# A fused attention and token-mixing kernel: one scaling product split, mix and projection steps of batch 0 and 2 reordered, a relu moved to GpSimd, three transposes in another tiling

## The chip, the cores and the metric

One core of one Trainium2 chip. The core has TensorE (PE, with its weight loads as PEld), VectorE (DVE), ScalarE (ACT), GpSimd (POOL) and SyncE (SP, which here issues every DMA). The metric is the device time of one execution in microseconds; a kernel's time is the median of its runs.

## The reference

Inputs are q, k and v of shape (8 batches, 8 heads, 576 positions, 64), and three weights. Everything is float32 outside the kernel. Per batch and head, a linear attention with a cosine weighting:

```python
def phi(x, c, s):                 # c, s = cos and sin of pi/2 * position / 576
    r = np.maximum(x, 0.0)
    return np.concatenate([r * c, r * s], axis=-1)
kv = np.einsum('bhsf,bhsd->bhfd', phi(k), v)
z = np.sum(phi(k), axis=2)
num = np.einsum('bhsf,bhfd->bhsd', phi(q), kv)
den = np.einsum('bhsf,bhf->bhs', phi(q), z)[..., None] + 1e-06
x = num / den                     # then (8, 576, 512): the heads side by side
```

and on x, per batch, a mixing of the positions and a projection:

```python
wq = x @ w_q;  wk = x @ w_k       # 512 -> 64
W_tok = scale * np.einsum('bsd,btd->bst', wq, wk)
mixed = np.einsum('bst,btd->bsd', W_tok, x)
out = np.maximum(mixed, 0.0) @ w_out
```

## The kernel before

The program is a list of steps in one string, `ORDER` (lines 26 to 67), which is read from left to right (lines 555 to 568). A word is a step's kind, a number, and up to three marks: `a` or `b` for one half of the data, `:n` for the first of the PSUM banks that it writes (for the steps of TensorE; OE's `:n` is an output buffer), `@A`, `@V` or `@G` for the engine (ScalarE, VectorE, GpSimd). So `KV6:2` is KV of group 6 into banks 2 and 3. Each engine executes its own steps in the order of the string; the steps of different engines are tied by semaphores where they share data, a buffer or a bank. Nothing is planned at run time.

The attention runs over 16 groups H, each with two pairs of heads (half a batch). For group H:

- LK, LQ, LV load k, q and v (line 145) into one of five raw buffers each, in halves of 288 KB.
- RK and RQ are the relus with a cast to bf16 (lines 203 and 205), CV casts v (209, 211).
- VS multiplies v by the cosine and sine table on VectorE (line 234; the tables and v both lie in SBUF). VG does the same on GpSimd straight from the raw data (248). Both write `v2`.
- KV contracts relu(k) with that product on TensorE (275 for the groups in `KV_WIDE`, 285 for the others), KE brings it to SBUF.
- QT transposes relu(q) on TensorE. For the groups in `QT_WIDE` (line 107) it is nine transposes of 128x128 (295), for the others 18 of 64 rows (301), with another layout in PSUM. QM multiplies the result by the q table on VectorE, as two products for a wide group (316) and as one for the others (320).
- N (two per group, 2H and 2H+1) multiplies by KV's result (340; some add the epsilon with two small matmuls, 348). EP, RC or RJ make the reciprocal of the denominator (357, 359, 378, 381), and X multiplies (393) and writes x.
- XT or XR transposes x on TensorE: XT with ten transposes of 128x128 (406), XR with 20 of 64 rows (419). XE brings the result to SBUF (213 on VectorE, 209 on ScalarE).

Per batch b, WK and WQ project (439, 452), KW and QW bring the results to SBUF, KX contracts x with wk (466), XK, XA and XB put it into place, and four mix products MX 4b to 4b+3 (489) follow, each with its evacuation and relu ME (500, 502). WO multiplies by w_out (509), OE brings the block of 128 rows to SBUF, ST stores it. KX of batch 2 uses the same buffers as that of batch 0, so the four MX of batch 0 come before XK2.

PSUM has eight banks. Most steps take a pair of them (`:0`, `:2`, `:4`, `:6`), WK, WQ, KX and WO a single one. A step of TensorE waits until the last step that used its banks has been read, so a bank number in `ORDER` is a dependency. Around the change, before it:

- MX6 4, XT4 0, MX7 2, QT6 6, N15 4, MX3 2, N14 0, WK2 6, WQ2 7, KV6 2, KX2 7, N13 2, N12 0, XR7 4, WO8 6 is TensorE's order with its banks. KV7, ahead of MX6, has banks 2 and 3, N8's, which X8 reads.
- VectorE: VS7, EP8, EP9, RJ4, X8, X9, QM7 (two), XE4, QM6 (two), VS6a, RC14, RC15, X14, X15, CW5, EP13, XK2.
- ScalarE: CV7a, KE4, RQ7a, ME5, ME4, RQ6a, XE5, KE7, ME6, ME7, RK6a, EP15, RK6b, ME3, KW2, QW2, KE6.
- GpSimd: CV7b, RQ7b, RK7, XB1, RQ6b, VG6b, CV6a, CV8a, CW4, CV8b, RQ8a, RK8a, RQ9a, RQ9b, RK9a, RK9b, VG11a. RK8b is on ScalarE.
- Near 56 us: KV8 into bank 0, KV9 into 6, MX9 into 4, MX11 into 0, N16 into 2, WQ3 into 6.

Of the kernel before, what the change touches and what calls it, by code (L numbers as in the profile page):

```python
# [27 lines left out]
LQ2a LK2a LW0 LV2a LQ2b LK2b TB TI TK TZ TQ RQ1a@G TW TV CV1@A VS1b RQ1b@A VS1a T2 QT1:0 RK1a@A  # L28
RK1b@V RQ0@V KV1:2 QM1 QT0:4 KE1@A CV0@G LV5b LV5a RK0@A LK5b LK5a LQ5a LQ5b LQ4b LQ4a N2:2 VS0 N3:0
VG3 QM0 KV0:6 KE0@A RC3 EP2@A X3 RQ3@A N0:6 N1:4 RC2 EP0@V EP1@V X2 RK3@A QT3:0 RC0 XT1:2 X0 XE1@A  # L30
RC1 X1 VG2b KV3:6 QM3 XR0:4 KE3@A CW1@A N6:0 XE0@V EP6@A N7:6 CW0@G EP7@A WK0:4 VG2a RQ2@A WQ0:5
KW0@V RC6 KX0:4 X6 RK2@A LK7a LV4a LV4b LK4a LK4b LV7a LV7b LQ7b LQ7a LQ6a LK7b LV6b LQ6b LW2 LK6b
LK6a LV6a LV8a LW3 LW4 LW5 LQ8b QT2:2 RC7 X7 CV5@A KV2:0 XK0@V QM2 XB0@G QW0@A XT3:6 KE2@A RK5@A
VS5a N5:0 WU5:2 N4:2 VS5b XE3@A RQ5@G EP5@V KV5:4 RC5 RC4 X5 XA0@A X4 QT5:6 KE5@A RQ4@G LQ9b LV8b
LQ8a MX0:0 QM5 XR2:2 ME0@A QT4:4 XE2@A N10:0 QM4 MX1:6 CV4@G LV9b LK8a LQ9a LV9a EP10@A ME1@A WK1:2
WQ1:3 RC10 KW1@A VS4 RK4@A LK9a LK8b LK9b KX1:2 MX2:6 N11:4 XK1@V QW1@A ME2@A EP11@V KV4:2 XA1@A
RC11 X10 CV7a@A CV7b@G X11 MX5:6 MX4:0 KE4@A RQ7b@G RQ7a@A VS7 N8:2 N9:4 ME5@A ME4@A QT7:6 RK7@G
EP8@V EP9@V RJ4 RQ6a@A XT5:0 X8 XB1@G XE5@A X9 KV7:2 RQ6b@G QM7 VG6b MX6:4 KE7@A XT4:0 ME6@A MX7:2
XE4@V QT6:6 ME7@A N15:4 QM6 RK6a@A MX3:2 N14:0 CV6a@G LV11a EP15@A RK6b@A WK2:6 ME3@A VS6a WQ2:7
KW2@A RC14 KV6:2 RC15 QW2@A X14 CV8a@G KX2:7 KE6@A CW4@G X15 CW2@A N13:2 CW3@A CW5@V N12:0 EP13@V  # L40
XR7:4 XK2@V WO8:6 RC13 XA2@A X13 EP12@A CV8b@G XE7@A WO2:7 RC12 VS8 WO7:2 CV9b@A RQ8a@G LQ13a LQ11b
LQ10a LK11b LK11a LQ11a LV11b X12 OE8:0@A MX8:4 WO6:3 RQ8b@A RK8a@G ME8@V OE7:1@A XR6:0 RQ9a@G WO1:6
CV9a@A XE6@V RQ9b@G OE2:2@A QT8:4 VS9 OE6:3@A RK8b@A QT9:0 RK9a@G OE1:4@A WK3:3 QM9 WO4:2 RK9b@G
KW3@A OE4:5@A ST4 LV12a LK10a LQ10b LV10a LV10b LQ12a KV8:0 QM8 XB2@A KV9:6 KE8@A MX9:4 KE9@A MX11:0
VG11a N16:2 ME9@A ME11@V WQ3:6 RC16 KX3:7 X16 QW3@A MX10:0 XK3@A N17:4 ME10@A N19:2 RK11@V N18:6
EP19@A WO11:0 EP17@V RQ11@A RC17 EP18@V X17 WO5:1 VG11b OE11:6@V ST11 LK12a LK10b LQ13b LV12b LK12b
LQ12b QT11:4 OE5:5@A RC19 RC18 X18 WO9:0 X19 WO10:1 OE9:7@A RQ10@G KV11:2 XA3@A QM11 XR8:6 KE11@A
XR9:4 VG10a LV15a LV13a LQ14b LV14b LQ14a LV13b XE8@A QT10:2 XE9@V WO0:5 QM10 OE10:8@A MX13:0
OE0:6@A MX12:6 N22:2 WO12:4 RQ13a@G ME12@V EP22@A XB3@A ME13@A RC22 VG10b WK4:5 X22 MX14:0 KW4@A
N23:6 ME14@V MX15:2 EP23@A KX4:5 RK10@A WQ4:0 XK4@V RQ13b@G RC23 WO3:1 ME15@A X23 XA4@G XB4@A QW4@A  # L50
RQ12b@G KV10:2 OE3:9@V RQ12a@A QT13:6 OE12:10@A ST12 LK13b LK13a LV14a VG12 MX18:0 WO14:5 QM13
KE10@A ME18@A XR11:2 OE14:11@A MX16:0 N21:6 XE11@V ME16@A N20:4 EP21@A EP20@V RK12@A QT12:0 RJ10 X21
WO16:2 RQ14b@A X20 WO13:3 QM12 VG13 XR10:4 OE13:10@A ST13 LK15b LK14b LK14a LV15b ST2 KV12:6 MX19:0
ME19@A WO17:3 OE16:12@A KE12@V XE10@V MX17:0 OE17:13@A N25:6 ME17@V N24:4 RQ14a@A WK5:3 EP25@V
# [16 lines left out]
def kernel(  # L71
# [32 lines left out]
    NUM_JOINT = ()  # L104
    WARM_COLS = 384
    VG_SPLIT = ()
    QT_WIDE = (0, 1, 2, 3, 4, 5, 6, 7, 8, 9, 10, 11, 14)
    KV_WIDE = (2, 4, 5, 7)

    pool = ctx.enter_context(tc.tile_pool(name="sb", bufs=1))  # L110
# [87 lines left out]
    A, V, G = nc.scalar, nc.vector, nc.gpsimd  # L198
# [59 lines left out]
    def qt_wide(i):  # L258
        return pair(i).rearrange("p t e -> p (t e)").bitcast(BF16)[:, 0:C * P].rearrange(
            "p (c n) -> p c n", c=C)  # L260
# [29 lines left out]
    def QT(H, ps, eng):  # L290
        place["QT", H] = ps
        if H in QT_WIDE:
            qt_v = qt_wide(ps)
# [18 lines left out]
    def QM(H, ps, eng):  # L312
        if H in QT_WIDE:
            q_t = qt_wide(place["QT", H]).rearrange("p c (r d) -> p r c d", r=2)
            for r in range(2):
                V.tensor_mul(  # L316
                    qm_b[H % NQM][:, :, r, 0:C, :],
                    q_t[:, r].unsqueeze(1).to_broadcast([P, 2, C, H2]), qtab)
            return
        V.tensor_mul(  # L320
            qm_b[H % NQM][:, :, :, 0:C, :].rearrange("p s r c d -> p s r (c d)"),
            qt_view(place["QT", H]).unsqueeze(1).to_broadcast([P, 2, 2, S]),
            qtab.rearrange("p s c d -> p s (c d)").unsqueeze(2).to_broadcast([P, 2, 2, S]))
# [275 lines left out]
```

## Time and profile before

| | |
|---|---|
| median of 3 runs | 119.17 us (118.6 to 119.84) |
| the profiled execution | 118.42 us |
| its span | 116.6 us |
| granted TensorE clock | 1.0 |
| DMA, share of 16 engines | 92.4% for the one queue of loads and stores |

The profile shows one execution. Times are in us from the start of the span. A row of a timeline has the start, the duration, the engine, the source line, the operation, output and inputs by name, shapes and the number of instructions merged, and in brackets the idle time of the engine ahead of it with the step that ended last before it began. The chain of waits follows back from the last instruction what released each step; its rows have start, duration, engine, name and line. Line numbers are those of the kernel below. The engines overlap the start of a step with the end of the one before by up to 0.1 us, so durations in a row add up to a little more than the time they take together.

### The profile page before, as it was taken

Reading aid. Unit: us, or ns where it says so; the run is one execution under the profiler, and the core shown is the slowest. Engines: PE = TensorE matmul, PEld = TensorE weight load, DVE = VectorE, ACT = ScalarE, POOL = GpSimd, SP = SyncE. Lnnn points to the kernel's source line nnn. Section 1 sums busy time; section 2 is a strip of 40 time slices with the busy share of each in tenths; the row PEclk is TensorE's granted clock in tenths of the full one; section 3 lists DMA queues with packets and bytes.
Section 4 is the critical chain, followed back from the end, with each engine's and each line's share of the span. In section 5 each row is a group of like instructions: output and inputs, shape, how many; then the busy total and the mean of one; then the engine's idle time right before and its main releaser. Section 6 shows DMA issues by size and latency. Waiting matters only on the chain.

```text
span 116.6 us, 4971 instructions
## 1 busy us (share of the span) xinstructions
PE 94.7 (81%) x2104; PEld 65.1 (56%) x2118; DVE 90.5 (78%) x162; ACT 83.1 (71%) x147; POOL 64.8 (56%) x65
## 2 busy tenths in 40 slices
PE   0005967779796797999999899999999999999970
PEld 0004856657576776647775656656775576463420
DVE  2008999799798999889799887898997996795620
ACT  4547558499899987898884878986888774546340
POOL 7600399861634796477298498899659901002000
PEclk9999999999999999999999999999999999999999
DMA  3999999999999999999979999987898467999874
GB/s 90 349 386 399 401 372 346 388 389 396 386 392 384 387 387 387 391 390 384 383 251 302 351 397 371 358 266 258 270 340 293 169 236 271 403 367 400 337 306 173
DMA packets 20662, 39.38 MB, mean 338 GB/s; under 512 B 3232, under 2 KB 3232, under 8 KB 20640
## 3 DMA queue, kind: packets, MB, share of 16 engines
q1 hardware_dynamic: 20640, 39.07, 92.4%
q8 instruction: 16, 0.26, 0.9%
q14 instruction: 6, 0.05, 0.1%
HBM read 29.62 MB, written 9.44 MB: 335 GB/s over the span
## 4 chain that ended last, share of the span: by engine, by line
PE 48%; DMA 26%; DVE 14%; SPq 4%; issue 3%; ACT 1%; DVEq 0%; ACTq 0%
PE ps L509 24%; DMA qraw<-in_q_dram 16%; DMA vraw<-in_v_dram 5%; DMA kraw<-in_k_dram 5%; PE ps L340 5%; DVE qm L316 5%; SPq L145 4%; PE ps L285 3%; PE ps L489 3%; PE ps L419 3%; PE ps L439 3%; DVE xT L213 3%; PE ps L466 3%; PE ps L452 2%; DVE x L393 2%
## 5 line engine op out<-in xcount | busy, mean ns | idle before, releaser
L248 POOL TENSOR_TENSOR v<-vraw,vtab 128x1152 bf16<-128x1152 f32 (+1 forms) x12 | 35.5, 2969 | 6.5 <-DVE qm L316 2.2
L509 PE MATMUL ps<-wow,mix 128*128 128x512 bf16 x130 | 33.3, 380 | 1.2 <-issue 0.3
L393 DVE TENSOR_TENSOR x<-ps,rec 128x640 bf16<-128x640 f32 x32 | 25.4, 818 | 0.7
L209 ACT COPY o<-ps 128x512 f32<-128x512 f32 x25 | 14.5, 592 | 9.2 <-PE ps L509 8.1
L509 PEld LDWEIGHTS <-mix 128*128 128x128 bf16 x144 | 12.5, 98 | 14.4 <-issue 1.7
L295 PE MATMUL ps<-ident,rq 128*128 128x128 bf16 x117 | 9.5, 233 | 12.0 <-ACT rq L203 11.0
L316 DVE TENSOR_TENSOR qm<-ps,qtab 128x1152 bf16<-128x1152 bf16 x26 | 18.3, 749 | 0.8 <-PE ps L295 0.7
L234 DVE TENSOR_TENSOR v<-vb,vtab 128x2304 bf16<-128x2304 bf16 (+1 forms) x11 | 11.8, 1084 | 7.7 <-ACT vb L209 7.3
L500 ACT ACTIVATE mix<-ps 128x576 bf16<-128x576 f32 x23 | 14.5, 651 | 3.5 <-PE ps L489 2.5
L340 PE MATMUL ps<-kvs,qm 64*128 64x65 bf16 x640 | 14.0, 193 | 2.1 <-ACT kvs L209 1.3
L295 PEld LDWEIGHTS <-rq 128*128 128x128 bf16 x117 | 7.6, 104 | 13.6 <-issue 10.5
L340 PEld LDWEIGHTS <-qm 64*128 64x128 bf16 x640 | 12.6, 96 | 4.2 <-issue 2.3
L203 ACT ACTIVATE rk<-kraw 128x1152 bf16<-128x1152 f32 (+1 forms) x14 | 14.0, 996 | 0.7 <-DMA kraw<-in_k_dram 0.7
L205 POOL TENSOR_SCALAR rq<-qraw 128x576 bf16<-128x576 f32 (+1 forms) x13 | 10.1, 776 | 4.4 <-DMA qraw<-in_q_dram 3.5
L211 POOL TENSOR_SCALAR vb<-vraw 128x576 bf16<-128x576 f32 (+1 forms) x7 | 5.7, 810 | 11.9 <-DMA vraw<-in_v_dram 8.8
L211 POOL TENSOR_SCALAR kx<-kx 64x256 bf16<-64x256 bf16 x9 | 4.1, 457 | 12.6 <-ACT kx L209 11.0
L502 DVE TENSOR_SCALAR mix<-ps 128x576 bf16<-128x576 f32 x9 | 6.8, 757 | 4.0 <-PE ps L489 3.8
L285 PE MATMUL ps<-v,rk 64*64 64x130 bf16 x432 | 9.1, 231 | 0.8 <-POOL v L248 0.7
L209 ACT CAST kvs<-ps 128x260 bf16<-128x260 f32 (+1 forms) x15 | 6.5, 436 | 4.6 <-PE ps L285 3.9
L285 PEld LDWEIGHTS <-rk 64*64 64x64 bf16 x432 | 7.5, 114 | 3.9 <-issue 1.2
L203 ACT ACTIVATE rq<-qraw 128x576 bf16<-128x576 f32 (+1 forms) x10 | 8.3, 832 | 1.1 <-DMA qraw<-in_q_dram 1.1
L213 DVE COPY xT<-ps 128x1280 bf16<-128x1280 bf16 (+1 forms) x9 | 7.3, 813 | 2.2 <-PE ps L419 2.0
(65 smaller groups left out, 137.3 us busy)
## 6 DMA issues: line engine op xcount, KB each, us to landing
kraw<-in_k_dram SPq DMA_DIRECT2D x32, 288.0 KB, 5.9
qraw<-in_q_dram SPq DMA_DIRECT2D x32, 288.0 KB, 5.9
vraw<-in_v_dram SPq DMA_DIRECT2D x32, 288.0 KB, 5.8
out_dram<-o SPq DMA_DIRECT2D x36, 256.0 KB, 3.4
wof<-in_moe_w_out_dram SPq DMA_DIRECT2D x4, 256.0 KB, 5.8
wkf<-in_moe_w_k_dram SPq DMA_DIRECT2D x1, 128.0 KB, 5.7
wqf<-in_moe_w_q_dram SPq DMA_DIRECT2D x1, 128.0 KB, 6.2
```

The costliest lines, as they stand in the source:

```text
L203: A.activation(dst, s, AF.Relu)
L209: A.copy(dst, s)
L213: V.tensor_copy(dst, s)
L234: V.tensor_mul(v2_b[H % NV2][:, part, :, :, 0:D], vb_b[H % NPREP][:, part].unsqueeze(3).to_broadcast([P, n, C, 2, D]), vtab.unsqueeze(1).t ...
L248: G.tensor_mul(dst[:, part, :, :, 0:D], s[:, part].unsqueeze(3).to_broadcast([P, n, C, 2, D]), vtab.unsqueeze(1).to_broadcast([P, n, C, 2, ...
L285: nc.tensor.matmul(kv_v[o, r, :], rk_of(H)[a, pr, c, :], v2_b[H % NV2][a, pr, c, :, 0:D + 1], start=(c == 0), stop=(c == C - 1))
L295: nc.tensor.transpose(qt_v[:, c, :], rq_b[H % NPREP][:, c, :, :], ident)
L316: V.tensor_mul(qm_b[H % NQM][:, :, r, 0:C, :], q_t[:, r].unsqueeze(1).to_broadcast([P, 2, C, H2]), qtab)
L340: nc.tensor.matmul(nv[:, pr, u, :], qm_b[H % NQM][a, s, r, 2 * u:2 * u + 2, :], kv_b[H % 2][a, r, pr if H in KV_WIDE else 0, s, 0:D + 1], ...
L393: V.tensor_tensor(x_b[b % NX][:, :, 4 * h:4 * h + 4, :].rearrange("p u (w r) d -> p r w u d", r=2)[:, r], nv[:, :, :, 0:D], rec(g).to_broa ...
L500: A.activation(dst, s, AF.Relu, scale=scale_moe)
L509: nc.tensor.matmul(o, mix_b[bp % 2][:, m, rt * P:(rt + 1) * P], wow[:, m, :], start=(m == 0), stop=(m == NDM - 1))
```

## The change

- VS7 becomes VS7b and VS7a, each half of the product.
- MX3 moves from behind N15 to behind XT4, and ME3 from behind RK6b to in front of ME7. WK2 moves from behind N14 to behind N15, and with it EP15 and RK6b in front of RK6a. Their banks, and those of 17 steps from MX7 to QT9 with them, change.
- RC14 moves behind KX2, X14 behind X15.
- MX9 moves from behind KV9 to behind N16, in front of ME9.
- RK8b goes from ScalarE to GpSimd, behind RQ9b and in front of RK9a.
- Group 0's transpose of x becomes XT0 instead of XR0; groups 6 and 10 leave `QT_WIDE`.

The same arithmetic is done. The diff, cut to the lines of `ORDER` that differ in more than their line breaks:

```diff
-RC1 X1 VG2b KV3:6 QM3 XR0:4 KE3@A CW1@A N6:0 XE0@V EP6@A N7:6 CW0@G EP7@A WK0:4 VG2a RQ2@A WQ0:5
+RC1 X1 VG2b KV3:6 QM3 XT0:4 KE3@A CW1@A N6:0 XE0@V EP6@A N7:6 CW0@G EP7@A WK0:4 VG2a RQ2@A WQ0:5
...
-RC11 X10 CV7a@A CV7b@G X11 MX5:6 MX4:0 KE4@A RQ7b@G RQ7a@A VS7 N8:2 N9:4 ME5@A ME4@A QT7:6 RK7@G
-EP8@V EP9@V RJ4 RQ6a@A XT5:0 X8 XB1@G XE5@A X9 KV7:2 RQ6b@G QM7 VG6b MX6:4 KE7@A XT4:0 ME6@A MX7:2
-XE4@V QT6:6 ME7@A N15:4 QM6 RK6a@A MX3:2 N14:0 CV6a@G LV11a EP15@A RK6b@A WK2:6 ME3@A VS6a WQ2:7
-KW2@A RC14 KV6:2 RC15 QW2@A X14 CV8a@G KX2:7 KE6@A CW4@G X15 CW2@A N13:2 CW3@A CW5@V N12:0 EP13@V
-XR7:4 XK2@V WO8:6 RC13 XA2@A X13 EP12@A CV8b@G XE7@A WO2:7 RC12 VS8 WO7:2 CV9b@A RQ8a@G LQ13a LQ11b
-LQ10a LK11b LK11a LQ11a LV11b X12 OE8:0@A MX8:4 WO6:3 RQ8b@A RK8a@G ME8@V OE7:1@A XR6:0 RQ9a@G WO1:6
-CV9a@A XE6@V RQ9b@G OE2:2@A QT8:4 VS9 OE6:3@A RK8b@A QT9:0 RK9a@G OE1:4@A WK3:3 QM9 WO4:2 RK9b@G
-KW3@A OE4:5@A ST4 LV12a LK10a LQ10b LV10a LV10b LQ12a KV8:0 QM8 XB2@A KV9:6 KE8@A MX9:4 KE9@A MX11:0
-VG11a N16:2 ME9@A ME11@V WQ3:6 RC16 KX3:7 X16 QW3@A MX10:0 XK3@A N17:4 ME10@A N19:2 RK11@V N18:6
+RC11 X10 CV7a@A CV7b@G X11 MX5:6 MX4:0 KE4@A RQ7b@G RQ7a@A VS7b VS7a N8:2 N9:4 ME5@A ME4@A QT7:6
+RK7@G EP8@V EP9@V RJ4 RQ6a@A XT5:0 X8 XB1@G XE5@A X9 KV7:2 RQ6b@G QM7 VG6b MX6:4 KE7@A XT4:0 MX3:2
+ME6@A MX7:6 ME3@A XE4@V QT6:4 ME7@A N15:0 EP15@A RK6b@A WK2:2 QM6 RK6a@A N14:6 CV6a@G LV11a VS6a
+WQ2:3 KW2@A KV6:4 RC15 QW2@A CV8a@G KX2:3 RC14 KE6@A CW4@G X15 X14 CW2@A N13:0 CW3@A CW5@V N12:6
+EP13@V XR7:4 XK2@V WO8:2 RC13 XA2@A X13 EP12@A CV8b@G XE7@A WO2:3 RC12 VS8 WO7:0 CV9b@A RQ8a@G LQ13a
+LQ11b LQ10a LK11b LK11a LQ11a LV11b X12 OE8:0@A MX8:4 WO6:1 RQ8b@A RK8a@G ME8@V OE7:1@A XR6:6 RQ9a@G
+WO1:0 CV9a@A XE6@V RQ9b@G OE2:2@A QT8:4 VS9 OE6:3@A RK8b@G QT9:6 RK9a@G OE1:4@A WK3:3 QM9 WO4:2
+RK9b@G KW3@A OE4:5@A ST4 LV12a LK10a LQ10b LV10a LV10b LQ12a KV8:0 QM8 XB2@A KV9:6 KE8@A KE9@A
+MX11:0 VG11a N16:2 MX9:4 ME9@A ME11@V WQ3:6 RC16 KX3:7 X16 QW3@A MX10:0 XK3@A N17:4 ME10@A N19:2
...
-    QT_WIDE = (0, 1, 2, 3, 4, 5, 6, 7, 8, 9, 10, 11, 14)
+    QT_WIDE = (0, 1, 2, 3, 4, 5, 7, 8, 9, 11, 14)
```

More of the change, by code (lines that the diff above doesn't have):

```diff
@@ L42 @@
-LQ10a LK11b LK11a LQ11a LV11b X12 OE8:0@A MX8:4 WO6:3 RQ8b@A RK8a@G ME8@V OE7:1@A XR6:0 RQ9a@G WO1:6
-CV9a@A XE6@V RQ9b@G OE2:2@A QT8:4 VS9 OE6:3@A RK8b@A QT9:0 RK9a@G OE1:4@A WK3:3 QM9 WO4:2 RK9b@G
-KW3@A OE4:5@A ST4 LV12a LK10a LQ10b LV10a LV10b LQ12a KV8:0 QM8 XB2@A KV9:6 KE8@A MX9:4 KE9@A MX11:0
-VG11a N16:2 ME9@A ME11@V WQ3:6 RC16 KX3:7 X16 QW3@A MX10:0 XK3@A N17:4 ME10@A N19:2 RK11@V N18:6
-EP19@A WO11:0 EP17@V RQ11@A RC17 EP18@V X17 WO5:1 VG11b OE11:6@V ST11 LK12a LK10b LQ13b LV12b LK12b
@@ L47 @@
[L47 to L51, printed above, removed]
+RC11 X10 CV7a@A CV7b@G X11 MX5:6 MX4:0 KE4@A RQ7b@G RQ7a@A VS7b VS7a N8:2 N9:4 ME5@A ME4@A QT7:6
@@ new lines @@
+WO1:0 CV9a@A XE6@V RQ9b@G OE2:2@A QT8:4 VS9 OE6:3@A RK8b@G QT9:6 RK9a@G OE1:4@A WK3:3 QM9 WO4:2
+RK9b@G KW3@A OE4:5@A ST4 LV12a LK10a LQ10b LV10a LV10b LQ12a KV8:0 QM8 XB2@A KV9:6 KE8@A KE9@A
+MX11:0 VG11a N16:2 MX9:4 ME9@A ME11@V WQ3:6 RC16 KX3:7 X16 QW3@A MX10:0 XK3@A N17:4 ME10@A N19:2
+RK11@V N18:6 EP19@A WO11:0 EP17@V RQ11@A RC17 EP18@V X17 WO5:1 VG11b OE11:6@V ST11 LK12a LK10b LQ13b
+LV12b LK12b LQ12b QT11:4 OE5:5@A RC19 RC18 X18 WO9:0 X19 WO10:1 OE9:7@A RQ10@G KV11:2 XA3@A QM11
+XR8:6 KE11@A XR9:4 VG10a LV15a LV13a LQ14b LV14b LQ14a LV13b XE8@A QT10:2 XE9@V WO0:5 QM10 OE10:8@A
@@ L52 @@
+MX13:0 OE0:6@A MX12:6 N22:2 WO12:4 RQ13a@G ME12@V EP22@A XB3@A ME13@A RC22 VG10b WK4:5 X22 MX14:0
+KW4@A N23:6 ME14@V MX15:2 EP23@A KX4:5 RK10@A WQ4:0 XK4@V RQ13b@G RC23 WO3:1 ME15@A X23 XA4@G XB4@A
+QW4@A RQ12b@G KV10:2 OE3:9@V RQ12a@A QT13:6 OE12:10@A ST12 LK13b LK13a LV14a VG12 MX18:0 WO14:5 QM13
 KE10@A ME18@A XR11:2 OE14:11@A MX16:0 N21:6 XE11@V ME16@A N20:4 EP21@A EP20@V RK12@A QT12:0 RJ10 X21
```

## The prediction

> **What bounds the kernel now.** I read the page first, then the busy time in two windows, then the chain of waits, then each engine's timeline between 36 and 58 us, where most of the edits lie.
>
> ```profile
> PE 94.7 (81%) x2104; PEld 65.1 (56%) x2118; DVE 90.5 (78%) x162; ACT 83.1 (71%) x147; POOL 64.8 (56%) x65
> ```
>
> ```profile
> 36.00:47.00 11.00, 8.94 (x232) 1.00 1.05 387
> 47.00:58.00 11.00, 10.71 (x243) 1.00 1.05 387
> ```
>
> The columns of the windows are the stretch, its length, TensorE busy, granted clock, share of the DMA engines and GB/s. TensorE is idle for 2.06 us of 36 to 47 and for 0.29 us of 47 to 58. So from 47 on TensorE itself is the path, and what the edits can win lies before 47. The DMA engines are full in both, so what waits for a landing does not come earlier. The chain of waits names the idle time:
>
> ```profile
> 42.41 0.76 DVE xT L213
> ...
> 43.19 1.43 DVE qm L316 x2
> ...
> 44.66 0.74 PE ps L439 x20
> 45.40 0.61 PE ps L452 x8
> 46.02 0.65 PE ps L285 x35
> 46.66 0.67 PE ps L466 x10
> 47.33 0.73 PE ps L340 x40
> 48.06 0.29 PE ps L419 x20
> ```
>
> Ahead of WK2 (44.66) it runs on VectorE, from VS7 over X8, X9 and QM7 to XE4 (42.41) and QM6 (43.19), and then through WQ2, KV6, KX2, N13 and N12, XR7 on TensorE. TensorE's own timeline shows the same from its side:
>
> ```profile
> 40.32 1.19 PE L275 MATMUL ps<-v,rk 64*128 64x260 bf16 x18 [0.32 <-DVE x L393]
> 41.34 0.30 PE L489 MATMUL ps<-wq,kx 64*128 64x288 bf16 x2
> 41.57 0.73 PE L406 MATMUL ps<-ident,x 128*128 128x128 bf16 x10
> 42.24 0.30 PE L489 MATMUL ps<-wq,kx 64*128 64x288 bf16 x2
> ```
> ```profile
> 44.66 0.74 PE L439 MATMUL ps<-wkw,xT 128*128 128x64 bf16 x20 [0.66 <-DVE qm L316]
> ```
>
> KV7 (40.32) waits 0.32 for X8, which empties its banks. WK2 (44.66) waits 0.66 for QM6: in this kernel WK2 writes the banks that held QT6, though it needs no number from it. VectorE:
>
> ```profile
> 37.59 1.36 DVE L234 TENSOR_TENSOR v<-vb,vtab 128x2304 bf16<-128x2304 bf16 x1 [0.42 <-ACT kvs L209]
> ```
> ```profile
> 44.52 0.75 DVE L234 TENSOR_TENSOR v<-vb,vtab 128x1152 bf16<-128x1152 bf16 x1
> ```
> ```profile
> 45.44 1.55 DVE L393 TENSOR_TENSOR x<-ps,rec 128x640 bf16<-128x640 f32 x2
> ```
>
> **The change, part by part. VS7 in two.** VS7 began 0.42 us after VectorE came free. Its two casts came from these:
>
> ```profile
> 35.51 0.67 POOL L211 TENSOR_SCALAR vb<-vraw 128x576 bf16<-128x576 f32 x1 [1.88 <-DVE rec L359]
> ```
> ```profile
> 36.40 0.67 ACT L209 CAST vb<-vraw 128x576 bf16<-128x576 f32 x1
> ```
>
> GpSimd's half was there at 36.18, ScalarE's at 37.07; VectorE came free at 37.17 (37.59 less 0.42). The row blames the next ScalarE step, which this product does not read, so the cause of the 0.42 is not clear. Split, the b half can start at 37.17, and two halves cost this:
>
> ```profile
> 9.15 1.43 DVE L234 TENSOR_TENSOR v<-vb,vtab 128x1152 bf16<-128x1152 bf16 x2 [7.30 <-ACT vb L209]
> ```
>
> 37.17 + 1.43 = 38.60 against 37.59 + 1.36 = 38.95: 0.35 earlier. If the stall stays whatever the split, it is 0.07 later. I take 0.35, since one half waits for nothing, and keep both ends. X8, X9 and QM7 follow without a gap, so KV7 moves to 39.97. It also waits for RK7:
>
> ```profile
> 38.52 1.44 POOL L205 TENSOR_SCALAR rk<-kraw 128x1152 bf16<-128x1152 f32 x1 [1.58 <-DMA kraw<-in_k_dram]
> ```
>
> This ends at 39.96 as it stands, part of it beside VS7, so 39.97 holds even if it gains nothing.
>
> **MX3 and WK2 ahead, and the other banks.** TensorE's order after XT4 becomes MX3, MX7, QT6, N15, WK2, N14, WQ2, KV6; ScalarE's becomes KE7, ME6, ME3, ME7, EP15, RK6b, RK6a. No step is added; no DMA is passed, for LV11a stays behind CV6a on SP and GpSimd. WK2 now waits for ME3, not for QM6. ScalarE's prices:
>
> ```profile
> 41.59 0.59 ACT L209 CAST kvs<-ps 128x520 bf16<-128x520 f32 x1 [0.44 <-PE ps L275]
> 42.08 1.20 ACT L500 ACTIVATE mix<-ps 128x576 bf16<-128x576 f32 x2
> 43.16 0.70 ACT L203 ACTIVATE rk<-kraw 128x576 bf16<-128x576 f32 x1
> 43.73 0.28 ACT L357 ACTIVATE rec<-ps,eps 128x10 f32<-128x10 f32 x1
> ```
>
> QT6 becomes 18 narrow transposes; these rows of the chain have the wide form and the narrow one:
>
> ```profile
> 62.44 0.50 PE ps L295 x9
> ```
> ```profile
> 73.75 0.37 PE ps L301 x18
> ```
>
> and QM6 one product instead of two:
>
> ```profile
> L320 DVE TENSOR_TENSOR qm<-ps,qtab 128x2304 bf16<-128x2304 bf16 x3 | 4.1, 1351 | 0.3 <-PE ps L301 0.3
> ```
>
> 1.35 against 1.43. Worked forward with these: KV7 39.97, MX6 40.99, XT4 41.22; KE7 ends about 41.83, so MX3 goes at 41.89 with no wait; MX7, which now needs QM7 gone (41.98), at 42.12; ME6 ends 42.39, QT6 42.44 to 42.81; XE4 42.0 to 42.78, N15 42.83 to 43.20; ME3 ends 42.96, so WK2 43.20 to 43.94, where it stood at 44.66. N14 with its two small matmuls about 0.45 to 44.39, WQ2 to 45.00. **What is late next** is KV6: it needs QM6 (42.85 to 44.20), VS6a after it (0.75, to 44.95) and RK6a, now last of ScalarE's seven: from 41.24, 0.49 for KE7 to the next start, 0.54 for each ME, 0.15 for EP15, 0.57 for RK6b and 0.70, 44.8. KV6 at 45.00 against 46.02 in the chain, then, with KX2 behind it, 46.32.
>
> **X14 behind X15.** N13 now uses N15's banks and N12 N14's, so each still waits for its own. The end of VS6a at 44.95, 0.17 to the first of the two products (45.27 to 45.44 in the rows above) and 1.55 for both put the end of X14 at 46.67. N13 starts at 46.32 and N12 at about 46.7, ending 47.07, where the chain had 48.06: 0.99 at XR7. I take 0.9, for the ends of steps are rounded here. If the stall of VS7 stays, VectorE's work from 37.59 to X14 is as long as it was to X15 (46.99) and N12 ends at 47.4: 0.6 less what the split costs, 0.5. If on the other side QM6, VS6a and the relus hid better, the idle time of 36 to 47 leaves no more than 1.5.
>
> **RK8b on GpSimd.** ScalarE loses 0.7 us that no step on the path waits for. GpSimd gets 0.67 more, in front of RK9a and RK9b, for which KV9 waits:
>
> ```profile
> 53.82 1.48 POOL L205 TENSOR_SCALAR rk<-kraw 128x576 bf16<-128x576 f32 x1 [0.72 <-DMA kraw<-in_k_dram]
> ```
> ```profile
> 53.43 1.35 DVE L234 TENSOR_TENSOR v<-vb,vtab 128x2304 bf16<-128x2304 bf16 x1
> ```
> ```profile
> 56.16 1.24 PE L285 MATMUL ps<-v,rk 64*64 64x130 bf16 x72
> ```
>
> RK9b took 1.48 instead of 0.67 while VS9 ran on VectorE (53.43 to 54.78): 0.52 of it lies behind VS9. RK8b's load is the one before RK9b's (53.82 by its wait), 0.7 us earlier at the full rate, so 53.1. With VS9 0.9 earlier (52.5 to 53.9) RK8b ends about 54.5, RK9a 55.2, RK9b 55.9. KV8 and KV9 are 0.62 each, so KV9 stood at 56.78 and now wants 55.88. It just fits: cost 0, at worst 0.3.
>
> By the Trainium skill, SBUF — State Buffer, Who interferes with whom, a VectorE product of two SBUF inputs and a GpSimd instruction that reads SBUF exclude each other for the whole instruction, whichever is first. RK9b would then end at 54.78 + 0.67 = 55.45; the trace has 55.30, so it nearly agrees. The same rule would move the sum if GpSimd came first, which is the second rival below.
>
> **The edits that I cost at nothing.** XT0 for XR0:
>
> ```profile
> 20.02 0.47 PE L419 MATMUL ps<-ident,x 64*128 64x64 bf16 x20
> 21.18 0.79 PE L340 MATMUL ps<-kvs,qm 64*128 64x65 bf16 x40 [0.70 <-DVE qm L316]
> ```
>
> Ten wide transposes take up to 0.73 (41.57 above) instead of 0.47, inside the 0.70 that TensorE waits for QM3; without that cover 0.26. QT10 narrow saves 0.13 into this wait:
>
> ```profile
> 66.93 1.02 PE L509 MATMUL ps<-wow,mix 128*128 128x512 bf16 x3 [0.31 <-DVE xT L213]
> ```
>
> so nothing, or 0.1 at QM10. MX9 behind N16 keeps TensorE's work the same; N17 waits for ME9, which takes 0.65, and behind MX9 now stand WQ3, KX3 and MX10 first, 0.61, 0.67 and 0.23. Without that cover it would cost 0.4, N16's length.
>
> **The sum.** 0.9 at XR7, 0 at KV9, and after it stores, loads and TensorE follow each other, so the end moves by the same 0.9. The profiled execution took 118.42 us, 116.6 of it the span: 117.5. It is 0.75 below the median of the runs shown, 119.17, so on that 118.3.
>
> **The rivals.** *VectorE swallows it.* The 0.42 in front of VS7 stays, and the chain XE4, QM6, VS6a, X15, X14, which no edit shortens by more than 0.08, stays the pole: gain 0 to 0.5, say 0.25: 118.9. For it: from XE4 on the chain above is VectorE's up to WK2, with gaps of 0.04 at most. Against it: 0.66 of TensorE's wait went to a bank, not to data.
>
> *GpSimd takes the port from VS9.* If VS9 is not running when RK8b's load lands (53.1), three relus go ahead of it back to back, 53.1 to 55.1 (3 x 0.67). VS9 then ends at 56.5 and QM9 (1.43), whose banks KV9 now takes, at 57.9, against 56.78 for KV9: 1.1 lost. QM8 behind it ends at 59.3, and N16, which waits for it, stood at about 57.9 (57.40 and two mix products of 0.23, as from 41.34 to 41.57): 1.4 lost. Less the 0.9 won earlier the end is 0.5 later: 119.7. It decides from a start of VS9 after 53.1. For it, a place where the trace shows GpSimd first:
>
> ```profile
> 85.34 0.67 POOL L205 TENSOR_SCALAR rk<-kraw 128x576 bf16<-128x576 f32 x1 [1.62 <-DMA kraw<-in_k_dram]
> ...
> 85.70 1.51 DVE L234 TENSOR_TENSOR v<-vb,vtab 128x2304 bf16<-128x2304 bf16 x1
> ```
>
> VS14 began inside that relu, which ends at 86.01, and took 0.16 longer than VS9's 1.35. Against it: VS9 should start at 52.5. The page of the Trainium skill named above is the rule by which this comes about; the two rows bear out half of it, for a whole block would cost 0.31.
>
> *More than the sum.* Waits behind 58 us (0.31 at 66.93 among them) shrink as well when VectorE and ScalarE come earlier: 1.4, so 117.8.
>
> **How the numbers follow.** Forecast 0.55, VectorE swallows it 0.20, GpSimd first 0.12, more than the sum 0.13. One per cent, 1.19 us, is about what a measurement of this kernel can tell from no change. The third case and over a quarter of the forecast's spread pass it: faster 0.30. Slower by as much takes the GpSimd case without the earlier gain, or something that I do not see: 0.09. The rest, 0.61, is within it. The range takes in the full idle time won (1.5) with a low run, 117.2, and half of the GpSimd case, 119.6; the forecast alone has 117.8 to 118.8.
>
> **What would show it.** Right: VS7 as two rows of 0.75 from 37.2; KV7 near 40.0; no wait for qm in front of WK2, which begins near 43.2; KV6 near 45.0; XR7 near 47.0; RK9b done before KV9. Wrong: VS7b still starting near 37.6; N12 waiting over 0.3 for X14; KV6 waiting for RK6a on ScalarE beyond 45.5; VS9 behind RK8b, or KV9 waiting for GpSimd; or all of these as said, and the end not moved, because a later stage gives it back.

## The result, and the profile after

The changed kernel takes 117.87 us (median of 22 runs, 117.18 to 119.31), the kernel before in the same runs 119.16 (22 runs, 118.24 to 120.64): ratio 0.9901, 95% interval 0.9879 to 0.9923. The profiled execution of the changed kernel took 117.66 us with a span of 115.9. A few slow or disturbed executions are left out of every ratio (so 0.9901 is not quite 117.87 over 119.16), and where the profiled execution was such a one (e3, at a granted clock of 0.868, and e6, at 189.06 us), its trace is not read.

The page's first part, and the two windows that the prediction began with:

```profile
PE 94.6 (82%) x2112; PEld 64.4 (56%) x2126; DVE 90.6 (78%) x161; ACT 82.5 (71%) x146; POOL 65.4 (56%) x66
```
```profile
36.00:47.00 11.00, 9.85 (x267) 7.90 (x265) 10.69 (x19) 10.16 (x21) 7.46 (x9) 1.00 1.05 390
47.00:58.00 11.00, 10.78 (x238) 6.99 (x234) 9.99 (x17) 9.07 (x19) 8.07 (x9) 1.00 1.05 387
```

The rows have stretch, length, then busy time of TensorE, its weight loads, VectorE, ScalarE and GpSimd, the clock, DMA share and GB/s. TensorE is idle for 1.15 us of 36 to 47, where it was 2.06: 0.91 us were won there. From 47 to 58 it is as full as before. VectorE's timeline:

```profile
35.86 1.50 DVE L393 TENSOR_TENSOR x<-ps,rec 128x640 bf16<-128x640 f32 x2
37.27 1.42 DVE L234 TENSOR_TENSOR v<-vb,vtab 128x1152 bf16<-128x1152 bf16 x2
...
43.08 1.36 DVE L320 TENSOR_TENSOR qm<-ps,qtab 128x2304 bf16<-128x2304 bf16 x1 [0.17 <-ACT mix L500]
```

The halves of VS7 stand behind X11 without a gap, where the whole product had 0.42 ahead of it. QM6 is one product. TensorE's timeline over the same stretch:

```profile
42.96 0.49 PE L340 MATMUL ps<-kvs,qm 64*128 64x65 bf16 x20
43.38 0.76 PE L439 MATMUL ps<-wkw,xT 128*128 128x64 bf16 x20
...
44.49 0.92 PE L452 MATMUL ps<-xT,wqw 128*64 128x288 bf16 x8
45.34 0.72 PE L285 MATMUL ps<-v,rk 64*64 64x130 bf16 x36
45.99 0.74 PE L466 MATMUL ps<-x,wk 128*64 128x256 bf16 x10
46.66 0.79 PE L340 MATMUL ps<-kvs,qm 64*128 64x65 bf16 x40
47.29 0.45 PE L419 MATMUL ps<-ident,x 64*128 64x64 bf16 x20
```

WK2 (43.38) follows N15 without a wait; before, it stood at 44.66 with 0.66 of idle time in front. KV6 is at 45.34 and XR7 at 47.29; TensorE's timeline before has them at 45.95 and 47.90. GpSimd near the moved relu, VectorE's VS9, and KV8 with KV9 on TensorE:

```profile
53.35 2.60 POOL L205 TENSOR_SCALAR rk<-kraw 128x576 bf16<-128x576 f32 x3 [0.71 <-DMA kraw<-in_k_dram]
```
```profile
52.82 1.35 DVE L234 TENSOR_TENSOR v<-vb,vtab 128x2304 bf16<-128x2304 bf16 x1
```
```profile
55.38 1.33 PE L285 MATMUL ps<-v,rk 64*64 64x130 bf16 x72
...
66.22 1.02 PE L509 MATMUL ps<-wow,mix 128*128 128x512 bf16 x3 [0.66 <-DVE xT L213]
```

VS9 runs first, and the three relus (RK8b, RK9a, RK9b) end at 53.35 + 2.60 = 55.95, in time for the two KV. The last row is WO0, whose wait for XE9 has grown from 0.31 to 0.66.

### The profile page after: what moved, and what is told of

It is laid out like the page before. It is cut to its first block, busy times and chain, and to the rows that moved or that the text cites. A ratio compares the mean times of both kernels' runs of the same rounds, so it can differ in the third digit from the quotient of the medians.

```text
span 115.9 us, 4985 instructions
## 1 busy us (share of the span) xinstructions
PE 94.6 (82%) x2112; PEld 64.4 (56%) x2126; DVE 90.6 (78%) x161; ACT 82.5 (71%) x146; POOL 65.4 (56%) x66
## 4 chain that ended last, share of the span: by engine, by line
PE 53%; DMA 26%; ACT 6%; DVE 5%; issue 3%; SPq 3%; ACTq 0%; DVEq 0%
PE ps L509 26%; DMA qraw<-in_q_dram 10%; DMA kraw<-in_k_dram 10%; DMA vraw<-in_v_dram 6%; PE ps L340 5%; PE ps L285 3%; PE ps L439 3%; PE ps L489 3%; SPq L145 3%; PE ps L419 3%; PE ps L466 3%; PE ps L452 3%; PE ps L295 2%; DVE xT L213 1%; DVE x L393 1%
## 5 line engine op out<-in xcount | busy, mean ns | idle before, releaser
L248 POOL TENSOR_TENSOR v<-vraw,vtab 128x1152 bf16<-128x1152 f32 (+1 forms) x12 | 35.0, 2926 | 4.4 <-PE ps L348 1.9
L295 PE MATMUL ps<-ident,rq 128*128 128x128 bf16 x99 | 8.1, 236 | 12.5 <-ACT rq L203 11.9
L234 DVE TENSOR_TENSOR v<-vb,vtab 128x1152 bf16<-128x1152 bf16 (+1 forms) x12 | 11.8, 1001 | 7.7 <-ACT vb L209 7.6
L316 DVE TENSOR_TENSOR qm<-ps,qtab 128x1152 bf16<-128x1152 bf16 x22 | 15.5, 749 | 0.5 <-ACT kvs L209 0.5
L295 PEld LDWEIGHTS <-rq 128*128 128x128 bf16 x99 | 6.6, 106 | 13.9 <-issue 10.8
L205 POOL TENSOR_SCALAR rq<-qraw 128x576 bf16<-128x576 f32 (+1 forms) x13 | 11.1, 859 | 4.5 <-ACT rk L203 2.6
L203 ACT ACTIVATE rk<-kraw 128x1152 bf16<-128x1152 f32 (+1 forms) x13 | 13.1, 1013 | 0.7 <-DVE rec L378 0.3
```

The source lines that it names most:

```text
L203: A.activation(dst, s, AF.Relu)
L205: eng.tensor_scalar(dst, s, FMAX, 0.0, op0=ALU.min, op1=ALU.max)
L234: V.tensor_mul(v2_b[H % NV2][:, part, :, :, 0:D], vb_b[H % NPREP][:, part].unsqueeze(3).to_broadcast([P, n, C, 2, D]), vtab.unsqueeze(1).t ...
L248: G.tensor_mul(dst[:, part, :, :, 0:D], s[:, part].unsqueeze(3).to_broadcast([P, n, C, 2, D]), vtab.unsqueeze(1).to_broadcast([P, n, C, 2, ...
L295: nc.tensor.transpose(qt_v[:, c, :], rq_b[H % NPREP][:, c, :, :], ident)
L316: V.tensor_mul(qm_b[H % NQM][:, :, r, 0:C, :], q_t[:, r].unsqueeze(1).to_broadcast([P, 2, C, H2]), qtab)
```

## The experiments

Up to 38 us the kernels have the same work but for XT0 and the halves of VS7, yet one execution stands up to 0.64 us behind another there. So steps of single executions are compared by their distance from the end of N8, a step of TensorE ahead of all other edits and with no wait for VS7. Ends in us, read from each trace instruction by instruction: the end of a step is that of its last matmul, and that of ST31, the last store, the end of its issue. Differences in the text are rounded only once.

| kernel | N8 | KV7 | XR7 | KV9 | KV11 | ST31 | that execution |
|---|---|---|---|---|---|---|---|
| before | 38.10 | +3.41 | +10.24 | +19.30 | +27.22 | +75.88 | 118.42 |
| changed | 38.23 | +3.03 | +9.52 | +18.49 | +26.39 | +74.99 | 117.66 |
| split alone (e1) | 38.58 | +3.01 | +9.86 | +19.17 | +26.95 | +75.66 | 118.72 |
| split alone, a first (e9) | 38.20 | +3.30 | +10.14 | +19.22 | +27.13 | +75.80 | 118.60 |
| VS7 whole (e2) | 37.99 | +3.40 | +9.79 | +19.34 | +27.32 | +76.26 | 118.72 |
| VS7 whole (e7) | 38.62 | +3.39 | +9.81 | +19.15 | +27.13 | +75.88 | 118.97 |
| VS7 whole, RK8b@A (e10) | 38.22 | +3.39 | +9.78 | +18.73 | +26.67 | +76.79 | 119.46 |
| core (e5) | 38.13 | +3.01 | +9.70 | +18.59 | +26.74 | +75.41 | 118.02 |
| RK8b@A (e4) | 38.17 | +3.01 | +9.41 | +18.30 | +26.28 | +74.88 | 117.50 |
| a first (e8) | 37.98 | +3.01 | +9.48 | +18.46 | +26.35 | +75.23 | 117.66 |
| wide again (e11) | 38.53 | +3.03 | +9.71 | +19.34 | +27.05 | +75.79 | 118.77 |
| X14 first (e12) | 38.23 | +3.01 | +9.72 | +18.70 | +26.59 | +75.56 | 118.25 |

Theory at the start: the split and the new order win at KV7 and at WK2 to XR7, and their gains add up. Rival: the one is worth nothing without the other, since a second wait stands right behind the one removed.

**The split alone.** The kernel before with one edit:

```diff
-VS7
+VS7b VS7a
```

> The kernel before with VS7 alone split into VS7b and VS7a. My sum: VS7b starts as VectorE comes free (0.42 us earlier than VS7 did), KV7 0.35 earlier, but WK2 still waits for QM6, so XR7 and the end come 0.35 earlier: ratio to before 0.997. If the split were all of the gain: ratio 0.990. If the stall ahead of VS7 stays whatever the form, or VectorE gives it back by 47 us: 1.000.

Ratio 0.9994, 0.9956 to 1.0032. KV7 ended 0.40 and XR7 0.39 earlier against N8; of that 0.22 is left at the end. TensorE around KV8 and KV9 in this execution:

```profile
56.25 1.51 PE L285 MATMUL ps<-v,rk 64*64 64x130 bf16 x72
```

These took 1.24 before. Nearly all of the difference is a stop inside KV9, at 57.1, where one matmul starts 0.27 us after the one before it; the trace has no semaphore for it.

**VS7 whole in the changed kernel.**

```diff
-VS7b VS7a
+VS7
```

> The changed kernel with VS7 whole again. My sum: the rest of the change alone, XR7 0.5 earlier than before, ratio 0.9955, and VS7 shows the stall of 0.4 us again; KV7 as late as before (40.3). If the split were all of the gain: 1.000. If the stall was chance and the split does nothing: 0.990, with VS7 starting as VectorE comes free.

Ratio 0.9988, 0.9948 to 1.0029. XR7 came 0.45 earlier than before, close to the 0.5 that the prediction gave for a stall that stays, but at KV9 nothing of it was left. The loads issued from 44 to 46.5 us (the columns are the count, KB each and the median us from issue to landing), first in this kernel and then in the changed one:

```profile
kraw<-in_k_dram SPq DMA_DIRECT2D x2, 288.0 KB, 6.9
qraw<-in_q_dram SPq DMA_DIRECT2D x1, 288.0 KB, 6.9
vraw<-in_v_dram SPq DMA_DIRECT2D x1, 288.0 KB, 7.0
```
```profile
vraw<-in_v_dram SPq DMA_DIRECT2D x2, 288.0 KB, 5.8
kraw<-in_k_dram SPq DMA_DIRECT2D x1, 288.0 KB, 5.7
qraw<-in_q_dram SPq DMA_DIRECT2D x1, 288.0 KB, 5.9
```

They land about 1.1 us later after issue. A load comes in sixteen shares, and fifteen of the sixteen of LK8a are there by 49.89, as in the other kernels; the last comes at 50.94, and a step waits for all sixteen. The load of v ahead of it has its last share at 50.33, 1.17 behind the other fifteen. ScalarE waits for that load to cast it and evacuates late, and TensorE waits at WO1, where no other kernel but e7 does:

```profile
50.41 0.67 ACT L209 CAST vb<-vraw 128x576 bf16<-128x576 f32 x1 [0.87 <-DMA vraw<-in_v_dram]
```
```profile
52.68 1.02 PE L509 MATMUL ps<-wow,mix 128*128 128x512 bf16 x4 [0.60 <-ACT o L209]
```

**The order alone.** The changed `ORDER` and banks with VS7 whole, RK8b on ScalarE, MX9 in its old place, XR0, groups 6 and 10 wide.

```diff
-VS7b VS7a ... XT0:4 ... RK8b@G ... MX9 behind N16, QT_WIDE without 6 and 10
+VS7 ... XR0:4 ... RK8b@A ... MX9 behind KE8, QT_WIDE with 6 and 10
```

> The kernel before with only the new order and banks (MX3, ME3, WK2, EP15, RK6b ahead, X14 behind X15): VS7 whole, RK8b on ScalarE, MX9 in its old place, XR0, groups 6 and 10 with wide transposes. My sum: as the changed kernel with VS7 whole, less 0.2 for the wide QT6 and QM6 at KV6: XR7 0.3 to 0.5 earlier than before, ratio 0.996 to 0.9975. If a part that I cost at nothing (RK8b, MX9, narrow tiles) carries the gain: 0.999 or more.

Ratio 0.999, 0.9956 to 1.0023. Its trace is not read, so this experiment has a time only.

**RK8b back on ScalarE** in the changed kernel.

```diff
-RK8b@G
+RK8b@A
```

> The changed kernel with RK8b on ScalarE as before. My sum: no difference to the changed kernel, ratio 0.990 within 0.002; RK9b is done near 55.3 instead of 55.95 and KV9 does not wait for it. If ScalarE's 0.7 us matter: 0.993 or more. If GpSimd's queue in front of KV9 holds the changed kernel back: 0.988 or less.

Ratio 0.9933, 0.9896 to 0.9969. This overlaps the whole change. KV9 came as early as there or earlier (+18.30 against +18.49), so the move shows neither a gain nor a cost there.

The first three left the parts alone near nothing, beside one per cent for the whole. Four more were to tell whether that is so.

**The core**: the changed kernel with the small edits undone, e3 with VS7 in two.

```diff
-VS7
+VS7b VS7a
```

> The split of VS7 and the new order of batch 0 with its banks, without the rest (RK8b stays on ScalarE, MX9 in its old place, XR0, groups 6 and 10 wide). If the rest costs and brings nothing, as the prediction had it, the ratio is that of the whole change, 0.988 to 0.992, and the first four KV9 steps and the relus of k move as they did there. If the rest (the narrow transposes of QT6 above all, which let QM6 be one product) is a part of the gain, 0.993 to 0.997.

Ratio 0.9952, 0.991 to 0.9994: the interval holds the whole second range (0.993 to 0.997) and touches the first (up to 0.992). Its trace says more: XR7 0.19 later than in the changed kernel, with QM6 as two products behind a wide QT6, and KV6 waiting 0.11 for VS6a, which it does not in the changed kernel. So the narrow QT6 has a share in the 0.73 won at XR7.

**The split alone, a second timing** of the kernel of the first experiment.

> The kernel before with VS7 in two, timed a second time because its first interval (0.9956 to 1.0032) holds both theories. Adds up: the 0.4 us that KV7 and XR7 came earlier stay to the end, 0.9965 (0.995 to 0.998). Only together: 0.9990 to 1.0010.

Ratio 1.0013, 0.998 to 1.0045. Its trace is not read.

**VS7 whole, a second timing** of the kernel of the second experiment.

> The changed kernel with VS7 whole, timed a second time (first 0.9948 to 1.0029). Its first profile came 0.48 us earlier at XR7 and lost that between 48 and 53 us, where one share of the loads of k and v landed 0.75 us late. Adds up, and that landing was chance: 0.996 (0.994 to 0.998), and in a profile without the late landing WO1 starts near 51.6 and KV9 near 56.1. Only together: 0.999 to 1.001, and WO1 late again although the loads land as in the changed kernel.

Ratio 0.998, 0.9946 to 1.0013. The late share is there again, from an earlier load on: the rows of the loads issued near 39.5 to 42.6 show 6.8 us, those of the changed kernel near 39.5 to 42.2 show 6.0. First this kernel:

```profile
qraw<-in_q_dram SPq DMA_DIRECT2D x2, 288.0 KB, 6.8
wof<-in_moe_w_out_dram SPq DMA_DIRECT2D x2, 256.0 KB, 6.8
```
```profile
qraw<-in_q_dram SPq DMA_DIRECT2D x2, 288.0 KB, 6.0
wof<-in_moe_w_out_dram SPq DMA_DIRECT2D x2, 256.0 KB, 5.9
```

The wait at WO1 is there too, 0.39.

**The halves the other way round** in the changed kernel.

```diff
-VS7b VS7a
+VS7a VS7b
```

> The changed kernel with VS7a in front of VS7b, so that the first half waits for ScalarE's cast, which ends at 37.1, and the second for GpSimd's. If what held the whole VS7 back for 0.4 us is the wait for ScalarE's cast, VS7a starts 0.4 after X11, KV7 comes 0.3 to 0.4 later and the ratio is 0.992 to 0.994. If it is the double wait of one instruction, on two engines, both halves start at once, VS7a 0.0 after X11, and the ratio is 0.990.

Ratio 0.9893, 0.9847 to 0.9939, not to be told from the whole change. VectorE here, and then in e7, where VS7 is whole:

```profile
35.47 1.50 DVE L393 TENSOR_TENSOR x<-ps,rec 128x640 bf16<-128x640 f32 x2
36.98 1.43 DVE L234 TENSOR_TENSOR v<-vb,vtab 128x1152 bf16<-128x1152 bf16 x2
```
```profile
36.21 1.49 DVE L393 TENSOR_TENSOR x<-ps,rec 128x640 bf16<-128x640 f32 x2
38.08 1.36 DVE L234 TENSOR_TENSOR v<-vb,vtab 128x2304 bf16<-128x2304 bf16 x1 [0.38 <-ACT kvs L209]
```

VS7a, which waits for ScalarE's cast alone, starts at once: 0.03 us after the end of that cast. So it isn't that cast which held the product back: with two halves, each waiting for one engine, there is no stall in either order, and with one product that waits for both there is one in all four traces that have it (0.42 before, 0.48 in e2, 0.38 in e7, 0.33 in e10).

**The split alone with a first.** The kernel before with `VS7a VS7b`.

> The kernel before with VS7a in front of VS7b, a third reading of the split alone. KV7 ends 0.38 earlier against N8, XR7 0.4 earlier. Only together, as the first two timings have it (0.9994 and 1.0013): 0.998 to 1.002. Adds up: 0.9967. If the loads of the next groups are what takes it back, the profile has one share of them landing 0.4 us or more behind the rest between 45 and 54 us.

Ratio 0.9984, 0.9948 to 1.0019. Here KV7 gained 0.11 only. GpSimd's RK7 and TensorE's KV7:

```profile
39.10 1.15 POOL L205 TENSOR_SCALAR rk<-kraw 128x1152 bf16<-128x1152 f32 x1 [2.18 <-DMA kraw<-in_k_dram]
```
```profile
40.31 1.19 PE L275 MATMUL ps<-v,rk 64*128 64x260 bf16 x18 [0.22 <-POOL rk L205]
```

RK7 started at 39.10, where it was 38.52 before, since its load landed late: the last share at 38.93, 0.66 behind the other fifteen. Between 45 and 54 us, where the expectation looked for such a share, none was 0.4 behind. It is the input that the prediction put at 39.96, 0.01 ahead of KV7: in an execution where that load is late, the second wait takes the place of the first.

**VS7 whole with RK8b on ScalarE** in the changed kernel, the edits of the second and the fourth experiment together.

> The changed kernel with VS7 whole and RK8b on ScalarE, a third reading of the order alone. XR7 0.45 earlier against N8. Adds up: 0.996 and, where the loads land without a straggler, KV9 0.4 earlier too. Only together: 0.998 to 1.000, with the loads again late by 0.7 us or more, or another wait at WO1, VS9 or KV9 that takes the 0.45.

Ratio 0.9933, 0.99 to 0.9967. XR7 and KV9 came 0.46 and 0.57 earlier than before. Then this execution lost more than that, on TensorE:

```profile
73.18 0.38 PE L301 MATMUL ps<-ident,rq 64*128 64x64 bf16 x14
74.25 0.23 PE L301 MATMUL ps<-ident,rq 64*128 64x64 bf16 x4 [0.69 <-issue]
...
90.18 0.36 PE L285 MATMUL ps<-v,rk 64*64 64x130 bf16 x11 [0.52 <-issue]
```

"issue" is a wait for nothing that the profile shows. It stands in the middle of a step, after 14 of 18 transposes.

**Groups 6 and 10 wide again** in the changed kernel.

```diff
-    QT_WIDE = (0, 1, 2, 3, 4, 5, 7, 8, 9, 11, 14)
+    QT_WIDE = (0, 1, 2, 3, 4, 5, 6, 7, 8, 9, 10, 11, 14)
```

> The changed kernel with groups 6 and 10 wide again. Costed at nothing by the prediction: 0.990. If QM6 as one product and its shorter way to KV6 are worth the 0.2 us that the core alone ended later at XR7: 0.992; the 0.2 us of the wide QT10 go into the wait in front of WO0 either way.

Ratio 0.9936, 0.9904 to 0.9967. XR7 0.20 later than in the changed kernel and KV6 with a wait of 0.11, as in the core. Behind KV8 the same kind of gap:

```profile
55.88 1.33 PE L285 MATMUL ps<-v,rk 64*64 64x130 bf16 x70
57.62 0.24 PE L285 MATMUL ps<-v,rk 64*64 64x130 bf16 x2 [0.41 <-issue]
```

**X14 in front of X15 again** in the changed kernel, RC14 in front of RC15.

```diff
-RC15 ... RC14 ... X15 X14
+RC14 RC15 ... X14 X15
```

> The changed kernel with X14 and RC14 in front of X15 and RC15, as before. N13, which now takes the banks of N15, then waits for the second product, which ends 0.75 later: N13 from 46.66 to about 47.3, N12 behind it and XR7 0.4 to 0.6 later, 0.994 to 0.995. If N13 has the time, no change, 0.990.

Ratio 0.9919, 0.9889 to 0.9949, and XR7 0.20 later than in the changed kernel. N13 waits as expected, for less:

```profile
44.49 0.68 PE L452 MATMUL ps<-xT,wqw 128*64 128x288 bf16 x8
45.15 0.72 PE L285 MATMUL ps<-v,rk 64*64 64x130 bf16 x36
...
46.87 0.79 PE L340 MATMUL ps<-kvs,qm 64*128 64x65 bf16 x40 [0.34 <-DVE x L393]
```

**What follows.** Weighted by their intervals, the split alone (three timings) is 0.9998, 0.9978 to 1.0018, and VS7 whole in the changed kernel (three) 0.9965, 0.9944 to 0.9985. Their product is 0.996 plus or minus 0.003, the whole change 0.990 plus or minus 0.002: over the runs the parts give more together than one by one. The three of VS7 whole do not agree well: e10, which also has RK8b on ScalarE, is at 0.9933 and the other two together at 0.998; with those two alone the product is 0.998 plus or minus 0.003. At XR7 the parts do not give more together: 0.39 (e1) and 0.45 (e2) would make 0.84, and it is 0.73. So the first theory holds up to 47 us and fails for the time. The rival's second wait is shown for one execution (e9, RK7), not for the others.

What the traces show behind XR7 is that single executions lose 0.2 to 1.5 us in places which no edit touches: a late share of the loads (e2, e7), TensorE stopping without a semaphore (e10, e11, inside KV9 in e1). Stops of TensorE in the middle of a step above 0.25 us are in none of the other traces between 40 and 74 us. Late shares (0.4 us or more behind the other fifteen) are in all twelve: in the changed kernel, too, the loads that land from 67.5 to 72.7 us have one 1.0 us behind. In e2 and e7 they fell on loads that the steps ahead of WO1 were waiting for. Whether that is chance or whether the new order makes it rarer stays open, and with it why the parts do not add up in the time. No other version beats the changed kernel by more than the intervals.

## Why the prediction was right, and where not

- **What bounds the kernel** was right: the idle time of 36 to 47 us was what could be won, and 0.91 us of its 2.06 were.
- **VS7 in two**: 0.38 at KV7 against N8, by the forecast's 0.35. The bound of 0.07 later "if the stall stays whatever the split" is out: in both orders the halves start without a gap. What the stall of the whole product is, which the prediction left open, is still open (see the last section).
- **WK2** at 43.38, with the execution 0.12 late at N8: 43.26, against 43.20. **KV6** was to start at 45.00: with the same 0.12 taken off it was 45.22 here, and 45.03 in e12, where TensorE has the same work up to there. The rest is in WQ2, whose row is 0.92 instead of e12's 0.68, with no wait shown.
- **XR7** came 0.73 earlier against N8, where 0.9 was taken; e4 had 0.84. The narrow QT6, which the prediction counted only by its durations, has 0.2 of it (e5, e11), and X14 behind X15 another 0.2 (e12), each by single executions.

**RK8b**: VS9 started at 52.82, ahead of the 53.1 at which the second rival decides, and the relus were done at 55.95 for the 55.9 worked out. KV8 and KV9 together take 1.33 instead of 1.24, so the fit is as close as was said. The rival's mechanism stands at another place, which the prediction did not name. GpSimd's RQ8a and VectorE's VS8 reach their start within 0.2 us of each other. In the changed kernel VS8 goes first:

```profile
49.02 1.73 POOL L205 TENSOR_SCALAR rq<-qraw 128x576 bf16<-128x576 f32 x1 [0.19 <-DMA qraw<-in_q_dram]
```
```profile
48.86 1.36 DVE L234 TENSOR_TENSOR v<-vb,vtab 128x2304 bf16<-128x2304 bf16 x1
```

and in e2 RQ8a:

```profile
48.61 0.67 POOL L205 TENSOR_SCALAR rq<-qraw 128x576 bf16<-128x576 f32 x1 [0.17 <-PE ps L509]
```
```profile
48.71 1.77 DVE L234 TENSOR_TENSOR v<-vb,vtab 128x2304 bf16<-128x2304 bf16 x1
```

Whichever is second is held while the first runs: 1.73 instead of 0.67, or 1.77 instead of 1.36. By the Trainium skill, SBUF — State Buffer, Who interferes with whom, the first to issue has the shared port for its whole instruction. Then RQ8a would end at 48.86 + 1.36 + 0.67 = 50.89 in the changed kernel and VS8 at 48.61 + 0.67 + 1.36 = 50.64 in e2; the rows end at 50.75 and 50.48, so they nearly agree.

- **QT10 narrow** brought nothing, as costed: the wait in front of WO0 grew from 0.31 to 0.66, and with QT10 wide (e5, e11) it is 0.31 as before.
- **The time.** On the profiled execution 117.5 was forecast and 117.66 measured. The step that failed is the next one, "It is 0.75 below the median of the runs shown, 119.17, so on that 118.3": the changed kernel's profiled execution is only 0.21 below its median (117.66 and 117.87). The term of 0.75 belongs to one execution and was 0.21 in the next. The 0.54 between them is more than the 0.43 from 118.3 to 117.87. In medians the change won 1.29 us, of which the two traces show 0.89 (at ST31 against N8); no trace shows the other 0.4. That these 0.89 are the 0.9 of the sum is in part luck: 0.73 of them are there at XR7, where 0.9 was taken, and 0.16 came behind it, where the sum had nothing.
- **"0.5 if the stall of VS7 stays"** held at XR7 (0.43 to 0.46 in e2, e7 and e10) and nearly for the time (0.9965 of 119.16 is 0.42 less, with e10 in it). That the split by itself would bring the other 0.4 did not hold.
- **The rivals.** VectorE did not swallow it, since the stall was gone. "More than the sum" named a number nearer to the median's gain, but its mechanism fell: the wait at WO0 did not shrink in any version.

## What to carry to other kernels

A short product that reads the results of two engines may be worth a trial in two halves, each waiting for one: here that took 0.4 us off VectorE's chain, though why the whole one starts late is open. A matmul step that writes a bank it needs nothing from is a wait that a reordering of banks removes. And one profiled execution is a draw: its distance to the median is not a constant to be added to a forecast, and gains of 0.4 us can be read at a step near the edit, but not at the end of one execution.

## What the runs showed of the hardware

**A late share stays late.** In e2 the sixteenth share of LK8a landed 1.05 us after the other fifteen, in e7 that of LW5 1.25 us after; both stayed behind for the loads that followed, with the DMA engines full. All twelve traces have such stretches, at different times, so what differs is which steps wait for those loads.

**TensorE stops in the middle of a step, perhaps for want of instructions.** The instruction packets of 16 KB take about 1 us of one DMA engine. In e11 the one that the changed kernel fetched between 50 and 54 us came between 55 and 56.5 instead, and TensorE stopped for 0.41 us at 57.2, inside a step and with no semaphore. In e1, with its stop at 57.1, that packet (the queue's seventh) started at 54.98; in the ten traces that have no stop there, between 52.0 and 53.1. The DMA rows of these two windows, first e11 (55 to 56.5), then the changed kernel (50 to 54), have packets, MB and the share of 16 engines:

```profile
q8 instruction: 1, 0.02, 4.5%
```
```profile
q8 instruction: 1, 0.02, 2.0%
```

4.5% of 16 engines for 1.5 us is 1.08 us on one. In e10 the stop of 0.69 us at 73.6 stands behind a packet that came between 71 and 73.5 us. That the late packet is the cause is argued from the order in time and not tested. The Trainium skill, Runtime: NRT & Kernel Launch, Instruction fetch mechanics, has an engine fetch its instructions in blocks of this size through a DMA queue of its own, at a cost that is mostly hidden. If these stops come from it, it was not hidden here.

**A product with two waits started late.** The whole VS7 waits for GpSimd's and for ScalarE's cast. Both were done when VectorE came free, yet it started 0.33 to 0.48 us later, in all four traces. In e7 ScalarE's cast and its next step are these:

```profile
36.92 0.67 ACT L209 CAST vb<-vraw 128x576 bf16<-128x576 f32 x1
37.49 0.59 ACT L209 CAST kvs<-ps 128x520 bf16<-128x520 f32 x1
```

The second one ends at 38.08, where VS7 starts, and the bracket of VS7's row names it. It cannot have released VS7 there: instruction by instruction, e7 has VS7's start at 38.081 and that step's semaphore at 38.091. The trace has one more instruction in front of the whole product, a wait of VectorE's sequencer for ScalarE, which the halves do not have. It ends 0.06 us after the cast, and the product starts 0.44 to 0.46 us after it (four traces). Two waits alone do not explain that: VS5a has the same pair of them, and started 0.04 us after its separate wait in the nine traces where VectorE was free. A rival is left: in the kernels with halves the second half stands at the whole product's place in VectorE's list, behind the first, which runs 0.75 us. So a delay that belonged to the place would be covered there. No run tells the two apart, and the mechanism is open.
